# Routing of the first MoE: token numbers kept in SBUF and stored once, half-width one-hots, gathers issued ahead of weights

## The chip, the cores and the metric

The kernel runs on one core of a Trainium2 chip. The metric is the device time of one execution in microseconds (us), as the median of several runs.

## The reference

Three stages run one after the other on 2 x 768 tokens of width 512 in float32: attention with 4 sink positions and a window of 128, a greedy mixture of experts (MoE), and a second MoE that mixes all experts with Sinkhorn weights. The change is in the greedy routing of the first MoE:

```python
logits = x @ w_gate                       # 1536 tokens, 8 experts
order = np.argsort(-logits.flatten())
for idx in order:                         # best (token, expert) pair first
    tok, e = idx // E, idx % E
    if assigned[tok] >= 0 or counts[e] >= cap:   # cap = 1536 / 8 = 192
        continue
    assigned[tok] = e; counts[e] += 1
for e in range(E):
    mask = assigned == e
    out[mask] = np.maximum(x[mask] @ w1[e], 0) @ w2[e]   # w1 512x1024, w2 1024x512
```

The second MoE takes `out` for all 1536 tokens; the kernel computes it in slot order (expert by expert) and scatters the rows to their tokens at the very end.

## The kernel before

Attention writes its rows to a DRAM tile `X` in chunks of 128 tokens and counts the first routing round along the way (`cnt0`). Then `routing_and_moe1` runs eight rounds. A round finds which expert fills up next and fixes its 192 tokens:

- `count(n, m, prop, row)` (L550 to L572) counts, for each token, how many tokens that propose the same expert stand before it. VectorE builds comparison matrices `g` and `gt` (L559 to L562, four buffers each, `GB = 4`), TensorE multiplies them with the proposals (L568), in groups of two chunks (`GC = 2`). There are n = 12 chunks in rounds 0 to 3 and, after `compact`, n = 6 in rounds 4 to 7. Round 0 takes `cnt0` and needs no count.
- `route(r)` (L574 to L606) picks the expert: `sel`, `red`, two small matmuls into `sm` (L590, L591), then `t1`, `eh`, `fin`, `ft`. At its end it strikes the expert and the placed tokens from `val` (L604, L605).
- `place_tokens(r, ...)` (L608 to L633) writes the expert's number to `EIX`, starts the weight loads (`load_w`, L648, 1 MB each, four for an expert: two halves of w1, two of w2), works out each token's slot (L611 to L613), builds one-hot rows `oh` of 192 columns (L617), multiplies them with the tokens' two-part number `code` (L622, a 2 x 192 result), folds the two parts and turns them to 96 partitions with four small matmuls against `pw` (L626, L629), casts them to the index tile `ix` (L631), and calls `gather`.
- `gather(r)` (L651 to L660) fetches 2 x 96 rows of `X` on the POOL queue (L657) and stores the 192 indices to the DRAM tile `idxd` on the SP queue (L660). Each index is an element of its own in DRAM, 4 bytes long.
- `propose()` (L527 to L546) makes the next round's proposals and spreads the values `m` along rows with TensorE (`bc`, L544) and ScalarE (`row`, L545).

`turn_tokens(r)` (L684 to L696) transposes the gathered rows into `xe`. `moe1(r)` (L698 to L733) multiplies: 64 instructions of L708 for w1, 64 of L719 for w2; half way through its L719 part it turns the tokens of round r + 1. The weights lie in six buffers of 1 MB (`WB = 6`). For round 0 w1 is loaded on the SP queue, w2 on the ACT queue after the last `row` copy (`st["shown"]`), and `turn_tokens(0)` is held until the third group of round 1's count (`KC = 2`).

A planner orders each engine's instructions from the program's order and its own costs. The routing has high priority; `tc.issue_after(x)` holds an instruction behind `x`. So routing of round r + 1 runs on VectorE while TensorE works on `moe1(r)`, and TensorE's order is fixed when the kernel is built.

`moe2` starts with a load of all indices from `idxd` to `ixo` (L793), used only by the scatters at the end (L875). Its weights come in halves of 512 KB on the SP queue (L437, L461), into three buffers (`SB = 3`), well ahead of use.

Of the kernel before, what the change touches and what calls it, by code (L numbers as in the profile page):

```python
# [20 lines left out]
def kernel(  # L21
# [21 lines left out]
    P = 128  # L43
# [27 lines left out]
    EIX = consts.tile([P, E], I32, name="EIX")  # L71

# [9 lines left out]
    slots = rp.tile([P, CAP], BF, name="slots")  # L82
    nc.vector.tensor_scalar(slots, place[:, :CAP], 5001.0, None, op0=OP.add)
# [4 lines left out]
    nc.gpsimd.iota(tok[:, :, 0], pattern=[[1, NCH]], base=0, channel_multiplier=0)  # L88
# [13 lines left out]
    HC = CAP // 2  # L102
    jw = rp.tile([2, 1], I32, name="jw")
    nc.gpsimd.iota(jw, pattern=[[0, 1]], base=P, channel_multiplier=1 - P)
    pw = rp.tile([2, 1], F32, name="pw")
    nc.vector.tensor_copy(pw, jw)
# [364 lines left out]
    def routing_and_moe1():  # L471
# [16 lines left out]
        IDX = {}  # L488
# [39 lines left out]
        def propose():  # L528
            n, L, val = st["n"], st["L"], st["val"]
            mx = rp.tile([P, n], F32, name="mx", bufs=2)  # L530
            prop = rp.tile([P, n, E], BF, name="prop", bufs=2)
            pl = rp.tile([P, n, E], F32, name="pl", bufs=2)
            m = rp.tile([P, n], F32, name="m", bufs=2)
            bc = lambda a: a.unsqueeze(2).to_broadcast([P, n, E])
            nc.vector.tensor_reduce(mx, val, axis=AX.X, op=OP.max)
            nc.vector.scalar_tensor_tensor(prop, val, 0.0, bc(mx), op0=OP.max, op1=OP.is_equal)
            nc.vector.tensor_mul(pl, prop, L)
            nc.vector.tensor_reduce(m, pl, axis=AX.X, op=OP.add)
            row = rp.tile([P, n, P], F32, name="row", tag="row", bufs=1)
            for c0 in range(0, n, 4):  # L540
                pb = ps.tile([P, 4, P], F32, name="bc", bufs=2)
                c1 = min(n, c0 + 4)
                for c in range(c0, c1):
                    nc.tensor.transpose(pb[:, c - c0, :], m[:, c:c + 1].to_broadcast([P, P]), ident)  # L544
                shown = nc.scalar.activation(row[:, c0:c1, :], pb[:, :c1 - c0], AF.Copy)  # L545
            st.update(row=row, m=m, prop=prop, shown=shown.ins)  # L546

        def count(n, m, prop, row):

            cnt = ps.tile([P, n, E], F32, name="cnt", bufs=1)  # L550
            nc.tensor.matmul(cnt.rearrange("p c e -> p (c e)"), zb, zb[:, :n * E], start=True, stop=False,
                             skip_group_check=True)
            for c0 in range(0, n, GC):
                c1 = min(n, c0 + GC)
                blocks = []
                for c in range(c0, c1):
                    g = gp.tile([P, n, P], BF, name="g", bufs=GB)
                    gt = gp.tile([P, P], BF, name="gt", bufs=GB)
                    nc.vector.scalar_tensor_tensor(gt, row[:, c], m[:, c:c + 1], before, op0=OP.is_equal, op1=OP.mult)  # L559
                    nc.vector.tensor_scalar(g[:, :c + 1], row[:, :c + 1], m[:, c:c + 1], None, op0=OP.is_lt)  # L560
                    if c + 1 < n:
                        nc.vector.tensor_scalar(g[:, c + 1:], row[:, c + 1:], m[:, c:c + 1], None, op0=OP.is_le)  # L562
                    blocks += [(c, gt, prop[:, c, :])] + [(cc, g[:, cc, :], prop[:, c, :]) for cc in range(n)]

# [6 lines left out]
                st.setdefault("counted", []).append(mm.ins)  # L571
            return cnt  # L572

        def route(r):  # L574
            n, L, val, code, m, prop = (st[x] for x in ("n", "L", "val", "code", "m", "prop"))
            bc = lambda a: a.unsqueeze(2).to_broadcast([P, n, E])
# [25 lines left out]
            ft = rp.tile([P, 2, n], F32, name="ft", bufs=2)  # L602
# [3 lines left out]
            return cnt, fin, ft, t1, code, n  # L606

        def place_tokens(r, cnt, fin, ft, t1, code, n):  # L608
            nc.vector.tensor_scalar(EIX[:, r:r + 1], t1[:, 1:2], -1.0, float(E), op0=OP.mult, op1=OP.add)
            load_w(r, (0,) if r == 0 else (0, 1))  # L610
            nc.vector.tensor_mul(fin, fin, cnt)  # L611
            nc.vector.tensor_reduce(ft[:, 1], fin, axis=AX.X, op=OP.add)
            nc.vector.tensor_add(ft[:, 1], ft[:, 0], ft[:, 1])  # L613
            sm = ps.tile([P, 512], F32, name="sm", bufs=1)
            ohs = gp.tile([P, n, CAP], BF, name="oh", bufs=OB)
            for c in range(n):
                nc.vector.tensor_scalar(ohs[:, c], slots, ft[:, 1, c:c + 1], None, op0=OP.is_equal)  # L617

            first = None
            for c in reversed(range(n)):  # L620
                with nullcontext() if first is None else tc.issue_after(first.ins):
                    mm = nc.tensor.matmul(sm[:2, :CAP], code[:, c, :], ohs[:, c], start=(c == n - 1), stop=(c == 0),  # L622
                                          skip_group_check=True)
# [8 lines left out]
            IDX[r] = ix  # L632
            gather(r)  # L633

        W, XG, YT = {}, {}, {}
        JH = KF // 2
        KC = 2
# [3 lines left out]
        def load_w(r, mats=(0, 1), q=nc.sync):  # L641
            e = q.value_load(EIX[0:1, r:r + 1], min_val=0, max_val=E - 1)
            for a in mats:
                src = (moe_w1, moe_w2)[a][bass.ds(e, 1)].rearrange("o (k p) f -> p (o k) f", p=P)
                for h in range(2):
                    t = bp.tile([P, WT], F32, name="wf", tag="w", bufs=WB)
                    t = t.rearrange("p (k f) -> p k f", f=DM if a else F // 2)
                    q.dma_start(t, src[:, h * KF // 2:(h + 1) * KF // 2] if a  # L648
                                else src[:, :, h * F // 2:(h + 1) * F // 2])
                    W.setdefault(r, ([], []))[a].append(t)  # L650

        def gather(r):
            ix = IDX[r]
            XG[r] = []
            for a in range(2):
                t = mp.tile([P, DM], F32, name=f"xg{a}", bufs=1)
                nc.gpsimd.indirect_dma_start(out=t[:HC], out_offset=None, in_=X[:, :],  # L657
                                             in_offset=bass.IndirectOffsetOnAxis(ap=ix[:, a:a + 1], axis=0))
# [26 lines left out]
        def turn_tokens(r):  # L685
# [3 lines left out]
            with tc.issue_after(st["counted"][KC]) if r == 0 else nullcontext():  # L689
                for k0 in range(0, KD, 2):  # L690
                    pt = pm.tile([P, 2, CAP], F32, name="mm", tag="mm", bufs=3)
                    for k in (k0, k0 + 1):
                        for a in range(2):
                            nc.tensor.transpose(pt[:, k - k0, a * HC:(a + 1) * HC], xg[a][:HC, k * P:(k + 1) * P],
                                                ident[:HC, :HC])
                    nc.scalar.activation(xe[:, k0:k0 + 2, :], pt, AF.Copy)  # L696

# [37 lines left out]
        for r in range(E):  # L735
            with tc.high_priority(offset=HP):
                got = route(r)
                place_tokens(r, *got)
                if r + 1 == E // 2:
# [10 lines left out]
            if r == 1:  # L750
                turn_tokens(0)
# [8 lines left out]
    def moe2(cx):  # L760
# [30 lines left out]
        acc = cp.tile([P, NCH, DM], F32, name="accs")  # L791
        ixo = cp.tile([P, NCH], I32, name="ixo")
# [146 lines left out]
```

## Time and profile before

| | |
|---|---|
| median of 3 runs | 1435.92 us (1433.2 to 1439.34) |
| the profiled execution | 1440.94 us |
| its span in the trace | 1439.2 us |
| TensorE busy in the span | 1394.8 us, 97% |
| mean granted TensorE clock | 0.979 of full speed |

The span runs from the first to the last instruction of the program; the profiled execution's time is 1.74 us longer. Attention takes the first 157 us, routing and the first MoE lie from 157 to about 415, the second MoE from there to the end. A granted clock of 1.00 is 2.4 GHz, 0.50 is 1.2 GHz.

### The profile page before, as it was taken

The page shows a single profiled execution, that of the slowest core. Times are in us where ns is not written, and L with a number is a line of the kernel's source. Part 1 is how long each engine was busy: PE and PEld are TensorE (multiplying, and loading weights), DVE is VectorE, ACT ScalarE, POOL GpSimd, SP SyncE. Part 2 cuts the span into 40 slices and gives each one's busy share as a digit, 9 for nine tenths or more (in the row PEclk, how much of TensorE's full clock was granted, in tenths as well). Part 3 has the DMA queues.
Part 4 walks back from the last instruction along what each step waited for, and adds up shares of the span by engine and source line. Part 5 has one row for each costly group of instructions (what it writes and reads, how often), then busy time and mean ns, then how long its engine had stood idle before and what let it go on. Part 6 is the DMA issues. An engine that isn't in the chain of part 4 may idle for free.

```text
span 1439.2 us, 20856 instructions
## 1 busy us (share of the span) xinstructions
PE 1394.8 (97%) x8275; PEld 1233.9 (86%) x8275; DVE 839.0 (58%) x1875; ACT 460.9 (32%) x975; POOL 412.0 (29%) x389
## 2 busy tenths in 40 slices
PE   7999589999989999999999999999999999999998
PEld 4667489999987988888898888888889888889887
DVE  4766767673156755555555555555555555555554
ACT  4566111221233322332333333233233333323321
POOL 1136200010252332243232234323223423222403
PEclk9999689999999999999999999999999999999999
DMA  6331453387620010011001001001100100100002
GB/s 128 94 82 38 87 185 129 129 182 152 224 59 15 30 44 30 30 41 34 30 30 45 30 31 44 30 30 41 34 30 30 45 30 30 44 30 30 15 1 88
DMA packets 87338, 87.39 MB, mean 61 GB/s; under 512 B 43976, under 2 KB 60360, under 8 KB 87240
## 3 DMA queue, kind: packets, MB, share of 16 engines
q1 hardware_dynamic: 82696, 74.50, 17.7%
q0 software_dynamic: 2944, 9.44, 3.2%
q10 hardware_dynamic: 1600, 2.11, 0.4%
q8 instruction: 65, 1.06, 0.3%
q14 instruction: 33, 0.27, 0.1%
HBM read 79.75 MB, written 6.30 MB: 60 GB/s over the span
## 4 chain that ended last, share of the span: by engine, by line
PE 91%; DVE 3%; DMA 2%; issue 2%; ACT 1%; POOL 0%; SPq 0%; POOLq 0%; DVEq 0%; ACTq 0%
PE pa L862 37%; PE X L805 18%; PE Z L805 9%; PE mm L719 5%; PE mm L708 5%; PE Y L805 5%; PE S L241 2%; DMA xg<-X,ix 2%; PE o L296 2%; PE PT L283 1%; PE ms L308 1%; PE cnt L568 1%; PE tr L217 1%; ACT pb L254 1%; PE lg L730 1%
## 5 line engine op out<-in xcount | busy, mean ns | idle before, releaser
L862 PE MATMUL pa<-w,h 128*128 128x512 f32 x2304 | 597.1, 395 | 0.0
L862 PEld LDWEIGHTS pa<-w,h 128*128 128x128 f32 x2304 | 427.7, 188 | 67.7 <-ACT h L812 0.3
L873 DVE SCALAR_TENSOR_TENSOR accs<-pa,Pm,accs 128x512 f32<-128x512 f32 x360 | 269.1, 747 | 212.0 <-PE pa L862 211.4
L813 DVE SCALAR_TENSOR_TENSOR h<-sum,h 128x384 fp32r<-128x384 f32 x192 | 156.1, 813 | 99.2 <-ACT h L812 99.0
L447 POOL TENSOR_TENSOR w1l<-r,w1h 128x512 fp32r<-128x512 f32 x64 | 64.6, 1031 | 446.0 <-ACT w1h L446 416.1
L812 ACT ACTIVATE h<-sum 128x384 fp32r<-128x384 f32 x192 | 100.4, 523 | 208.0 <-DVE sum L822 207.9
L464 POOL TENSOR_TENSOR w<-r,w 128x1024 fp32r<-128x1024 f32 x32 | 77.3, 2417 | 232.8 <-ACT w L463 232.8
L817 ACT ACTIVATE u<-X 128x384 f32<-128x384 f32 x64 | 31.5, 492 | 268.6 <-PE X L805 268.6
L708 PE MATMUL mm<-xe,wf 128*128 128x192 f32 x512 | 96.6, 340 | 0.0
L719 PE MATMUL mm<-hT,wf 128*128 128x192 f32 x512 | 96.0, 337 | 0.0
L447 POOL TENSOR_TENSOR w1l<-S,w1h 128x1024 fp32r<-128x1024 f32 x32 | 86.9, 2714 | 0.0
L708 PEld LDWEIGHTS mm<-xe,wf 128*128 128x128 f32 x512 | 84.9, 195 | 0.9 <-issue 0.3
L719 PEld LDWEIGHTS mm<-hT,wf 128*128 128x128 f32 x512 | 84.5, 194 | 0.8 <-issue 0.2
L657 POOL DMA_INDIRECT xg<-X,ix x16 | 16.3, 1020 | 192.6 <-DVE ix L631 126.7
L822 DVE TENSOR_TENSOR sum<-Z,u 128x384 f32<-128x384 f32 x64 | 35.7, 557 | 58.8 <-ACT u L817 58.8
L817 ACT ACTIVATE v<-X 128x384 f32<-128x384 f32 x64 | 31.4, 491 | 78.0 <-PE X L805 78.0
L254 ACT ACTIVATE pb<-pb,nb 128x264 f32<-128x264 f32 (+1 forms) x96 | 46.4, 488 | 14.5 <-DVE nb L249 13.3
L813 DVE SCALAR_TENSOR_TENSOR h<-X,h 128x384 fp32r<-128x384 f32 x64 | 35.7, 558 | 21.8 <-ACT h L812 21.8
L822 DVE TENSOR_TENSOR sum<-Z,v 128x384 f32<-128x384 f32 x64 | 35.7, 557 | 18.6 <-PE Z L805 18.5
L812 ACT ACTIVATE h<-X 128x384 fp32r<-128x384 f32 x64 | 31.5, 492 | 46.0 <-PE X L805 45.9
L446 ACT ACTIVATE w1h<-r 128x512 fp32r<-128x512 f32 x64 | 30.0, 516 | 49.3 <-PE Z L805 46.2
L244 DVE CUSTOM_DVE_ANT_0 pb<-S,M 128x264 f32<-128x264 f32 (+1 forms) x96 | 36.5, 403 | 14.4 <-PE S L241 13.7
(284 smaller groups left out, 2362.0 us busy)
## 6 DMA issues: line engine op xcount, KB each, us to landing
r<-in_moe_w_dram SPq DMA_DIRECT2D x64, 512.0 KB, 3.5
wf<-in_moe_w_dram SPq DMA_DIRECT2D x30, 1024.0 KB, 5.4
kn<-in_k_dram SPq DMA_DIRECT2D x12, 256.0 KB
qn<-in_q_dram SPq DMA_DIRECT2D x12, 256.0 KB, 4.4
vn<-in_v_dram SPq DMA_DIRECT2D x12, 256.0 KB, 3.1
X<-xs POOLq DMA_DIRECT2D x12, 256.0 KB, 2.6
wf<-in_moe_w_dram ACTq DMA_DIRECT2D x2, 1024.0 KB
xg<-X,ix POOLq DMA_INDIRECT x16, 8.2
```

Of the source, the lines that this page charges most:

```text
L254: nc.scalar.activation(PB[c][:, h, :w], PB[c][:, h, :w], AF.Exp, bias=NB[c][:, 0, h:h + 1], scale=scale, accum_out=NB[c][:, 2, h:h + 1])
L447: nc.gpsimd.tensor_sub(w1[1][:, o:o + n], x, w1[0][:, o:o + n].bitcast(F32))
L464: nc.gpsimd.tensor_sub(w2[:, 1], r2, w2[:, 0].bitcast(F32))
L708: nc.tensor.matmul(ph[:, j - j0, :], w1[j // JH][:, k, j % JH * P:(j % JH + 1) * P], xe[:, k, :], start=(k == 0), stop=(k == KD - 1))
L719: nc.tensor.matmul(py[:, k - k0, :], w2[j // JH][:, j % JH, k * P:(k + 1) * P], hT[:, j, :], start=(j == 0), stop=(j == KF - 1))
L805: nc.tensor.matmul(acc_, w1[a][:, o, k, :], XO[x][t][b][:, k, :], start=(start and n == 0), stop=(stop and n == 3 * KH - 1), skip_group_ch ...
L812: nc.scalar.activation(t[:, 0], x, AF.Relu)
L813: nc.vector.scalar_tensor_tensor(t[:, 1], x, 0.0, t[:, 0].bitcast(F32), op0=OP.max, op1=OP.subtract)
L817: nc.scalar.activation(t, x, AF.Copy)
L822: nc.vector.tensor_add(t, a, b)
L862: nc.tensor.matmul(pa, HT[u, f, h][:, a, j * P:(j + 1) * P], w2[:, b, f, :], start=(n == 0), stop=(n == 3 * FP - 1))
L873: nc.vector.scalar_tensor_tensor(acc[:, c], pa, pe, acc[:, c], op0=OP.mult, op1=OP.add)
```

## The change

Six edits, all around the routing:

1. The one-hots have 96 columns. A token's slot is split into its half (`ft[:, 1]`, 0 or 1) and its place in the half (`ft[:, 2]`). The one-hots stand as weights on TensorE and the token numbers move past them, four columns for each chunk (`ch`: two parts of the number, for each half). The result lies on 96 partitions at once: a reduction adds the two parts and a cast writes `ixs[:, r, :]`. The copy `fi`, the four matmuls against `pw` and the tile `pw` are gone. `code` holds 128 x chunk in its first part, so no factor is needed.
2. The slot number comes from `fin = (cnt + 1) * fin`, built in `route`; two operations and an addition in `place_tokens` are gone.
3. The eight stores to `idxd` are gone. `moe2` stores all 1536 indices once, ahead of the load to `ixo`.
4. In rounds 1 to 7 the gathers stand ahead of the weight loads, which are held until the indices are known. In round 0 the first half of w1 is loaded ahead; the other three halves are on the ACT queue after the last `row` copy.
5. The striking of expert and tokens from `val` is a function of its own (`leave`), after the placing.
6. On TensorE the `bc` transposes are held behind the placing matmuls; `turn_tokens(0)` is called in round 0 and held behind the last `bc` transpose, and round 1's count is held behind it.

```diff
         nc.vector.scalar_tensor_tensor(fin, cnt, float(CAP) - 0.5, prop, op0=OP.is_lt, op1=OP.mult)
+        nc.vector.scalar_tensor_tensor(fin, cnt, 1.0, fin, op0=OP.add, op1=OP.mult)
...
-        nc.vector.scalar_tensor_tensor(val, be(eh), -100.0, val, op0=OP.mult, op1=OP.add)
-        nc.vector.scalar_tensor_tensor(val, bc(ft[:, 0]), -1000.0, val, op0=OP.mult, op1=OP.add)
...
-        nc.vector.tensor_scalar(EIX[:, r:r + 1], t1[:, 1:2], -1.0, float(E), op0=OP.mult, op1=OP.add)
-        load_w(r, (0,) if r == 0 else (0, 1))
-        nc.vector.tensor_mul(fin, fin, cnt)
-        nc.vector.tensor_reduce(ft[:, 1], fin, axis=AX.X, op=OP.add)
-        nc.vector.tensor_add(ft[:, 1], ft[:, 0], ft[:, 1])
+        if r == 0:
+            expert()
+            load_w(0, ((0, 0),))
+        nc.vector.tensor_scalar(ft[:, 1], ft[:, 0], HC + 0.5, None, op0=OP.is_gt)
+        nc.vector.scalar_tensor_tensor(ft[:, 2], ft[:, 1], -float(HC), ft[:, 0], op0=OP.mult, op1=OP.add)
         sm = ps.tile([P, 512], F32, name="sm", bufs=1)
-        ohs = gp.tile([P, n, CAP], BF, name="oh", bufs=OB)
+        ohs = gp.tile([P, n, HC], BF, name="oh", bufs=OB)
         for c in range(n):
-            nc.vector.tensor_scalar(ohs[:, c], slots, ft[:, 1, c:c + 1], None, op0=OP.is_equal)
+            nc.vector.tensor_scalar(ohs[:, c], slots, ft[:, 2, c:c + 1], None, op0=OP.is_equal)
+        ch = gp.tile([P, n, 2, 2], BF, name="ch", bufs=OB)
+        nc.vector.tensor_mul(ch[:, :, 1], code, ft[:, 1].unsqueeze(2).to_broadcast([P, n, 2]))
+        nc.vector.tensor_sub(ch[:, :, 0], code, ch[:, :, 1])
...
-                mm = nc.tensor.matmul(sm[:2, :CAP], code[:, c, :], ohs[:, c], start=(c == n - 1), stop=(c == 0),
-                                      skip_group_check=True)
+                mm = nc.tensor.matmul(sm[:HC, 0:4], ohs[:, c], ch[:, c].rearrange("p h a -> p (h a)"),
+                                      start=(c == n - 1), stop=(c == 0), skip_group_check=True)
...
-        fi = rp.tile([2, CAP], F32, name="fi", bufs=2)
-        nc.vector.tensor_copy(fi, sm[:2, :CAP])
-        sm = ps.tile([P, 512], F32, name="sm", bufs=1)
-        for a in range(2):
-            nc.tensor.matmul(sm[:HC, a:a + 1], fi[:, a * HC:(a + 1) * HC], pw, start=True, stop=True)
-        ix = rp.tile([HC, 2], I32, name="ix", bufs=3)
-        nc.vector.tensor_copy(ix, sm[:HC, 0:2])
+        st["placed"] = mm.ins
+        at = rp.tile([HC, 2], F32, name="at", bufs=2)
+        nc.vector.tensor_reduce(at, sm[:HC, 0:4].rearrange("p (h a) -> p h a", h=2), axis=AX.X, op=OP.add)
+        known = nc.vector.tensor_copy(ixs[:, r, :], at)
         gather(r)
+        if r:
+            with tc.issue_after(known.ins):
+                expert()
+            load_w(r, PARTS)
...
+    def leave(ft, eh, n):
+        val = st["val"]
+        nc.vector.tensor_scalar(ft[:, 3], ft[:, 0], 0.5, None, op0=OP.is_gt)
+        nc.vector.scalar_tensor_tensor(val, eh.unsqueeze(1).to_broadcast([P, n, E]), -100.0, val, op0=OP.mult,
+                                       op1=OP.add)
+        nc.vector.scalar_tensor_tensor(val, ft[:, 3].unsqueeze(2).to_broadcast([P, n, E]), -1000.0, val,
+                                       op0=OP.mult, op1=OP.add)
...
-        nc.sync.dma_start(idxd[r * CAP:(r + 1) * CAP, :].rearrange("(a p) o -> p (a o)", p=HC), ix)
...
             place_tokens(r, *got)
+            leave(got[0], got[2], got[4])
...
                 with tc.issue_after(st["shown"]):
-                    load_w(0, (1,), nc.scalar)
+                    load_w(0, PARTS[1:], nc.scalar)
+                turn_tokens(0)
...
-        if r == 1:
-            turn_tokens(0)
...
     acc = cp.tile([P, NCH, DM], F32, name="accs")
+    nc.sync.dma_start(idxd.rearrange("(r a p) o -> p (r a o)", a=2, p=CAP // 2), ixs.rearrange("p r a -> p (r a)"))
     ixo = cp.tile([P, NCH], I32, name="ixo")
     nc.sync.dma_start(ixo, idxd.rearrange("(c p) o -> p (c o)", p=P))
```

## Rows read from the trace of the kernel before

**Rows 1.** The page: busy time, share of the span, instructions.

```profile
PE 1394.8 (97%) x8275; PEld 1233.9 (86%) x8275; DVE 839.0 (58%) x1875; ACT 460.9 (32%) x975; POOL 412.0 (29%) x389
```

**Rows 2.** Windows: one expert's stretch; length, busy by engine, granted clock, DMA share, GB/s.

```profile
347.10:369.65 22.55, 22.55 (x146) 22.43 (x146) 1.19 (x3) 4.65 (x11) 2.57 (x3) 1.00 0.82 238
```

**Rows 3.** Chain that ended last, 130 to 460 us: start, length, what.

```profile
162.77 2.25 DVE oh L617 x12
165.06 2.08 PE sm L622 x12
...
169.11 10.02 DMA xg<-X,ix
...
202.44 7.66 DMA xg<-X,ix
...
211.36 0.67 PE cnt L568 x26
212.29 4.30 PE mm L719 x14
...
217.22 2.06 PE mm L719 x12
...
233.67 1.08 PE sm L622 x12
...
235.44 0.42 PE sm L629 x4
...
291.33 0.59 PE sm L622 x6
```

**Rows 4.** Timeline of round 0, 150 to 232 us: start, length, instruction.

```profile
160.97 0.24 DVE L603 TENSOR_REDUCE ft<-fin 128x12 f32<-128x96 f32 x1
...
162.78 1.08 SPq L648 DMA_DIRECT2D wf<-in_moe_w_dram  x2
...
168.67 0.15 DVE L631 CAST ix<-sm 96x2 int32<-96x2 f32 x1 [1.15 <-PE sm L629]
...
169.69 0.35 DVE L559 SCALAR_TENSOR_TENSOR gt<-row,m,before 128x128 bf16<-128x128 f32 x1 [0.87 <-ACT row L545]
...
170.40 0.60 ACT L545 ACTIVATE row<-bc 128x512 f32<-128x512 f32 x1 [0.25 <-PE bc L544]
...
170.45 0.93 POOL L657 DMA_INDIRECT xg<-X,ix  x1 [0.30 <-issue]
...
171.96 0.98 ACTq L648 DMA_DIRECT2D wf<-in_moe_w_dram  x2
...
182.33 2.93 PE L708 MATMUL mm<-xe,wf 128*128 128x192 f32 x8
```

**Rows 5.** DMA queues, 171 to 180 us: packets, MB, share of 16 engines.

```profile
q0 software_dynamic: 101, 0.33, 74.6%
q10 hardware_dynamic: 57, 0.12, 8.4%
```

**Rows 6.** DMA queues, 365 to 369 us.

```profile
q0 software_dynamic: 128, 0.39, 33.2%
```

**Rows 7.** Line L660, the eight stores to idxd: issue to landing.

```profile
DMA to landing us min/median/max: 11.0/11.9/12.7
```

**Rows 8.** Timeline of TensorE: its waits for gathered rows in moe1(0) and moe1(1).

```profile
208.00 0.30 PE L694 MATMUL mm<-ident,xg 96*128 96x96 f32 x1 [1.65 <-DMA xg<-X,ix]
210.14 1.22 PE L694 MATMUL mm<-ident,xg 96*128 96x96 f32 x6 [1.84 <-DMA xg<-X,ix]
...
245.09 0.80 PE L694 MATMUL mm<-ident,xg 96*128 96x96 f32 x7 [0.86 <-DMA xg<-X,ix]
```

**Rows 9.** Timelines of SP and ACT in the second MoE.

```profile
424.99 0.50 SPq L793 DMA_DIRECT2D ixo<-idxd  x1
...
451.33 0.37 SPq L461 DMA_DIRECT2D r<-in_moe_w_dram  x1
...
500.99 1.06 ACT L463 ACTIVATE w<-r 128x1024 fp32r<-128x1024 f32 x1 [0.89 <-PE pa L862]
```

More of the change, by code (lines that the diff above doesn't have):

```diff
@@ L81 @@
     nc.vector.tensor_copy(place, ji)
-    slots = rp.tile([P, CAP], BF, name="slots")
-    nc.vector.tensor_scalar(slots, place[:, :CAP], 5001.0, None, op0=OP.add)
+    HC = CAP // 2
+    slots = rp.tile([P, HC], BF, name="slots")
+    nc.vector.tensor_scalar(slots, place[:, :HC], 5001.0, None, op0=OP.add)
     je = rp.tile([P, E], I32, name="je")
@@ L543, in propose @@
                 for c in range(c0, c1):
-                    nc.tensor.transpose(pb[:, c - c0, :], m[:, c:c + 1].to_broadcast([P, P]), ident)
+                    with tc.issue_after(st["placed"]):
+                        spread = nc.tensor.transpose(pb[:, c - c0, :], m[:, c:c + 1].to_broadcast([P, P]), ident)
                 shown = nc.scalar.activation(row[:, c0:c1, :], pb[:, :c1 - c0], AF.Copy)
-            st.update(row=row, m=m, prop=prop, shown=shown.ins)
+            st.update(row=row, m=m, prop=prop, shown=shown.ins, spread=spread.ins)
         def count(n, m, prop, row):
             cnt = ps.tile([P, n, E], F32, name="cnt", bufs=1)
-            nc.tensor.matmul(cnt.rearrange("p c e -> p (c e)"), zb, zb[:, :n * E], start=True, stop=False,
-                             skip_group_check=True)
+            turned = st.pop("turned", None)
+            with nullcontext() if turned is None else tc.issue_after(turned):
+                nc.tensor.matmul(cnt.rearrange("p c e -> p (c e)"), zb, zb[:, :n * E], start=True, stop=False,
+                                 skip_group_check=True)
             for c0 in range(0, n, GC):
@@ L601, in route, with place_tokens, expert @@
             nc.vector.tensor_mul(fin, fin, be(eh))
[L602 removed]
+            ft = rp.tile([P, 4, n], F32, name="ft", bufs=2)
             nc.vector.tensor_reduce(ft[:, 0], fin, axis=AX.X, op=OP.add)
[L604 to L613 removed]
+            return ft, t1, eh, code, n
+        def place_tokens(r, ft, t1, eh, code, n):
+            def expert():
+                return nc.vector.tensor_scalar(EIX[:, r:r + 1], t1[:, 1:2], -1.0, float(E), op0=OP.mult, op1=OP.add)
+            if r == 0:
[3 more added lines that the diff above has]
+            nc.vector.scalar_tensor_tensor(ft[:, 2], ft[:, 1], -float(HC), ft[:, 0], op0=OP.mult, op1=OP.add)
             sm = ps.tile([P, 512], F32, name="sm", bufs=1)
[L615 removed]
+            ohs = gp.tile([P, n, HC], BF, name="oh", bufs=OB)
             for c in range(n):
[L617 removed]
+                nc.vector.tensor_scalar(ohs[:, c], slots, ft[:, 2, c:c + 1], None, op0=OP.is_equal)
+            ch = gp.tile([P, n, 2, 2], BF, name="ch", bufs=OB)
+            nc.vector.tensor_mul(ch[:, :, 1], code, ft[:, 1].unsqueeze(2).to_broadcast([P, n, 2]))
+            nc.vector.tensor_sub(ch[:, :, 0], code, ch[:, :, 1])
             first = None
@@ L635, in routing_and_moe1, with load_w @@
         W, XG, YT = {}, {}, {}
         JH = KF // 2
-        KC = 2
+        PARTS = ((0, 0), (0, 1), (1, 0), (1, 1))
         GC, GB = 2, 4
         OB = 1
-        def load_w(r, mats=(0, 1), q=nc.sync):
+        def load_w(r, parts, q=nc.sync):
             e = q.value_load(EIX[0:1, r:r + 1], min_val=0, max_val=E - 1)
-            for a in mats:
+            for a, h in parts:
                 src = (moe_w1, moe_w2)[a][bass.ds(e, 1)].rearrange("o (k p) f -> p (o k) f", p=P)
[L645 to L650, printed above, removed]
+                t = bp.tile([P, WT], F32, name="wf", tag="w", bufs=WB)
+                t = t.rearrange("p (k f) -> p k f", f=DM if a else F // 2)
+                q.dma_start(t, src[:, h * KF // 2:(h + 1) * KF // 2] if a else src[:, :, h * F // 2:(h + 1) * F // 2])
+                W.setdefault(r, ([], []))[a].append(t)
@@ L688, in turn_tokens @@
             xe = XE[r] = mp.tile([P, KD, CAP], F32, name="xe", bufs=1)
-            with tc.issue_after(st["counted"][KC]) if r == 0 else nullcontext():
+            with tc.issue_after(st["spread"]) if r == 0 else nullcontext():
                 for k0 in range(0, KD, 2):
```

22 lines of the change are left out of this document (7 added, 15 removed).

## The prediction

> **What bounds the kernel now.** I read the page first: TensorE is busy for 97% of the span [rows 1]. That is an average, so I went to the windows of one expert at a time: from 347 to 370 us, where no routing is left, TensorE is busy for all of its 22.55 us at the full clock [rows 2]. There only less work on TensorE helps. Then I read the chain that ended last over the routing stage. Round 0 is different: the chain runs through VectorE's one-hots, the placing matmuls and then 10.02 us of one gather [rows 3]. The timeline shows the first matmul of the first MoE only at 182.33 us, 8 of them taking 2.93 us, the half clock [rows 4]. TensorE's own timeline names its last waits: 1.65 and 1.84 us for round 1's rows, 0.86 us for round 2's [rows 8]. Behind the first two, 14 matmuls take 4.30 us, where 12 take 2.06 a little later [rows 3]: the clock fell to its lower level after the wait. So a gain can come from three places: the start at 182.33 us, these waits, and TensorE's routing work.
>
> **Why the gather of round 0 takes 10 us.** The queues from 171 to 180 us tell it. The gather's queue moves 0.33 MB and keeps the engines for 74.6% of 9 us; the weights that ACT issued at 171.96 us move 0.12 MB [rows 4, 5]. In round 7 a whole gather of 0.39 MB takes 33.2% of 4 us [rows 6]: for each MB 3.4 us of all engines instead of 20. What differs: in round 0 the 192 single-index stores went out just ahead of the gather, and such a store takes 11.0 to 12.7 us to land [rows 7], so until about 180 us. Round 7's gather has no store ahead of it. My reading is that the stores in flight slow all that comes behind, the gather and w2 alike.
>
> **Round 0, step by step.** The count's `ft` is reached at 160.97 + 0.24 = 161.2 us as before; the added (cnt + 1) * fin falls into VectorE's wait for the `sm` matmuls. Now the one-hots begin at 162.77 [rows 3, 4]. After the change two short dependent operations stand between, about 0.2 us each like `ft`: one-hots from 161.65. Twelve take 2.25 us [rows 3], 0.19 each; at half the width each lies between half of that and the same, I take 0.15: 1.8 us, to 163.45. The two operations on `ch`: 0.35, to 163.8. The placing matmuls become 12 short ones with 4 columns. Nearest are the count's 26 in 0.67 us at full clock [rows 3], so 0.3 us, double at the lower clock; the old 2.08 us is the upper bound. I take 0.6: 164.4. Reduction and cast take the place of copy, fold and cast, two VectorE operations, 0.4 us: 164.8. Before, the cast ended at 168.67 + 0.15 = 168.8. So indices come **4.0 us earlier**.
>
> The gathers start at 165.1 and, 1.3 us apart as before (169.11 and 170.45) [rows 3, 4], 166.4. With no store in flight I price a gather by round 7, within 4 us [rows 6], and take 3: rows at 169.4 us. The other bound is the old price, 170.45 to about 181, which is a rival below. ACT comes next: the last `row` copy ended at 171.0 [rows 4]. The proposals start after the placing as before, the first `g` on VectorE moves from 169.69 [rows 4] to about 167.1, so the last copy ends at 168.4. ACT needed 1.0 us to issue the first load and 0.98 for two, so three are out at 170.9, and only then does it copy `xe`. The first matmul of moe1(0) starts at 172.0 instead of 182.33: **-10.3 us**. Between -8 (ACT or the gather a little late) and -12 (the copies planned ahead of the loads). The second half of w1 is now behind the gather: issued at 169.4, it needs to be there after 32 matmuls at 0.17 to 0.37 us [rows 3, 4], after 177 us at the earliest, so it is hidden if the ACT queue flows at once.
>
> **Rounds 1 and later.**
> Gather waits of round 1: the count starts 2.6 us earlier, isn't held up by much else, and the same savings between `sel` and the indices are about 2.4 us. By this the rows of round 1 come about 12 us earlier than at 210.1, and TensorE, which is 10.3 us ahead, needs them about when they come. Of 1.65 + 1.84 us I leave 0.5: **-3.0**. With the wait gone the half clock behind it goes too, 14 matmuls at 2.06/12 are 2.4 instead of 4.30: **-1.9**. Round 2's 0.86 us: **-0.9** [rows 3, 8].
> TensorE's work: L622 takes 1.08 us in rounds 1 to 3 and 0.59 in rounds 4 to 7 [rows 3]; new 0.31 and 0.15 by the count's price. 3 x 0.77 + 4 x 0.44 = 4.1. The four fold matmuls go, 0.42 in each of 7 rounds [rows 3]: 2.9. Together **-7.0**, all on the path, since TensorE is the bound there.
> Against it: three of round 1's six count groups ran while TensorE waited for round 0's rows. Now all stand behind `turn_tokens(0)`, 3 x 0.67: **+2.0**. VectorE holds four `g` buffers, so it works on for some 5 us past 167.1 and isn't stopped before the count begins at about 170.6.
> Costed at nothing: `leave` and the extra VectorE operations (as many go as come, and VectorE idles while TensorE multiplies); weights later by some 6 us in rounds 1 to 7, since 1 MB halves already wait for a free buffer in most rounds, and round 1's are needed only at about 207 us; without these covers each late half would stop TensorE for as long as it is late.
>
> **The store at the second MoE.** It is 1536 single elements, issued at about 404 us (424.99 less 21), and the load to `ixo` waits for it on SP. Behind it in SP's queue stands the w2 half of 451.33, which ACT first uses at 500.99 [rows 9]. So SP can be held for some 70 us at no cost. Nothing in the trace has so many stores in one; lower bound, one old store's 11 to 13 us (hidden), upper bound eight of them, 88 to 102 us [rows 7]. The old stores went to one 768-byte piece each, these go to all pieces at once, so I take the low end.
>
> **Sum.** -10.3 - 3.0 - 1.9 - 0.9 - 7.0 + 2.0 = -21.1 us. From the profiled execution's 1440.94 that is 1419.8. It lies 5.0 us above the median 1435.92; the median after comes to **1415 us**, 1.5% faster.
>
> **Rivals.**
> *Gather stays slow.* The 10 us belong to the first gather and not to the stores. Then the rows come at 177 us, the start moves by 4 us only: 1421 us. For it: in round 1 a gather takes 7.66 us too [rows 3]. Against: that one had 4 MB of weights ahead, and round 7. Chance 0.14.
> *Order is worth nothing.* In round 1 the gather's packets still share the engines with weights that are issued 1 us later; wait and lower clock stay: 3.0 + 1.9 back, 1420 us. The Trainium skill, DMA: Bandwidth & Descriptors, section "Issuing engines are not separate DMA queues", says that DMAs of all issuing engines run on the same 16 and interleave. By that rule the order of issue buys little here; the 7.66 us agree with it. Chance 0.15.
> *The one store is slow.* It costs by the element: 88 to 102 us hold SP from 404 to 492 or 506. The w2 half then comes 16 to 30 us after ACT wants it, and ACT, in order, stops the products: 1431 to 1445 us. From 93 us on it takes more than the 21 that were won, and the kernel is slower; at 102 by 0.6%. It would be worse if the planner issued it early among the last weights. The Trainium skill, same page, "Specifications", speaks for it: below 512 B a write is a read-modify-write. By that each of the 1536 pays, and the estimate is the upper end. Rows 7 agree that single elements are dear, and can't say whether the price adds up. Chance 0.11.
> *The planner's order.* Tokens of round 0 ahead of the count hold TensorE and the count longer than thought, or the lower clock comes back elsewhere at 2 us a time: 1423 to 1434 us. Chance 0.08.
>
> **From cases to numbers.** The forecast has 0.52 (own range 1408 to 1421; the low side is a start 12 us earlier and no wait at all). A measurement here can tell about 0.5%, 7 us, from no change. Faster by more (under 1428.7): 0.52 + 0.14 + 0.15 and half of the last case, 0.85. Within it: half of the store's case and the rest of the last, 0.09. Slower: 0.06, the store's upper end. For 8 in 10 the range takes in the two near rivals and the last one's lower part, 1404 to 1430.
>
> **What would show it.** Right: gathers of round 0 landing within 4 us, the first L708 near 172 us, no wait for `xg` over 0.5 us in moe1(0), no 14-matmul stretch of 4.3 us behind it, the placing groups at 0.3 and 0.15 us, no gap on SP that reaches ACT's L463. Wrong: a gather that still takes 10 us, ACT's loads that sit 8 us in their queue, or SP standing at `ixo` while weights are due.

## Result, and the profile after

After the change the kernel takes **1415.21 us** (median of 4 runs, 1413.82 to 1420.05) against 1435.48 us for the kernel before on the same chip: ratio 0.9862, interval 0.9843 to 0.988. The profiled execution has a span of 1413.8 us where that of before has 1439.2. The 25.4 us between these two spans are looked for below; the medians differ by 20.3, so some 5 us of what the two traces differ by belongs to the two executions.

The busy line of the page of the changed kernel:

```profile
PE 1375.5 (97%) x8243; PEld 1221.7 (86%) x8243; DVE 835.5 (59%) x1898; ACT 459.8 (33%) x975; POOL 411.8 (29%) x388
```

TensorE has lost 19.3 us of work against [rows 1], so most of the gain is work or lower clock that is gone and not idle time. Where it went is read from the windows of one expert at a time. First before, moe1(0), moe1(1) and moe1(4), and the first 45 us of the second MoE (columns: window, its length, busy time of TensorE, its weight loads, VectorE, ScalarE, GpSimd with counts, granted clock, DMA share, GB/s):

```profile
182.33:221.03 38.70, 35.21 (x355) 33.35 (x354) 24.91 (x75) 6.13 (x13) 2.20 (x2) 0.87 0.43 151
221.03:253.70 32.67, 31.81 (x363) 30.32 (x363) 25.05 (x76) 6.76 (x14) 2.20 (x2) 1.00 0.42 142
...
316.60:347.10 30.50, 30.50 (x226) 28.70 (x227) 16.86 (x71) 7.07 (x16) 1.93 (x2) 0.94 0.79 150
414.48:460.00 45.52, 39.01 (x184) 34.12 (x184) 35.59 (x88) 17.34 (x34) 17.73 (x15) 0.87 0.13 35
```

And the same stretches of the changed kernel, with the one ahead of its first matmul of moe1(0):

```profile
157.00:177.00 20.00, 9.36 (x136) 7.93 (x137) 16.45 (x58) 2.66 (x5) 1.96 (x2) 0.50 0.59 207
177.09:208.41 31.32, 31.32 (x358) 30.25 (x355) 26.93 (x83) 5.73 (x12) 1.83 (x2) 0.95 0.44 162
208.41:239.46 31.05, 31.05 (x364) 30.05 (x364) 24.46 (x80) 6.82 (x15) 1.98 (x2) 1.00 0.44 150
...
297.46:323.65 26.19, 26.19 (x212) 25.80 (x212) 13.26 (x53) 6.74 (x16) 4.75 (x6) 1.00 0.67 203
...
391.01:436.00 44.99, 38.39 (x188) 33.31 (x188) 35.75 (x89) 17.34 (x34) 17.70 (x15) 0.93 0.13 36
```

moe1(0) starts 5.2 us earlier (177.09 for 182.33), is 7.4 us shorter and without a gap on TensorE (31.32 busy in 31.32; 35.21 in 38.70 before). These windows end up to 0.9 us off an expert's first w1 matmul; counted from first w1 matmul to first w1 matmul, moe1(0) is 7.7 us shorter, moe1(1) to moe1(4) are 2.0, 2.1, 2.1 and 4.3 us shorter, and the last three experts the same. In moe1(4) the clock was 0.94 and is 1.00. The rest of the span is some 2 us shorter, its first 45 us at clock 0.93 instead of 0.87.

Of the 5.2 us, 2.3 are none of the change's: the routing's first reduction on TensorE (`sm<-red`) begins at 156.36 instead of 158.64, and that moment lies between 154.8 and 159.0 in the profiles of all the kernels here, with edits that don't touch what stands ahead of it. So the start is worth 3.0 us (23.7 us behind the routing's start before, 20.7 now), not 10.3. The timeline of that stretch shows why:

```profile
163.31 0.16 DVE L632 CAST ixs<-at 96x2 int32<-96x2 f32 x1
164.32 1.03 POOL L668 DMA_INDIRECT xg<-X,ixs  x1 [9.33 <-DVE m L534]
165.66 0.93 POOL L668 DMA_INDIRECT xg<-X,ixs  x1 [0.30 <-issue]
168.39 1.52 ACTq L661 DMA_DIRECT2D wf<-in_moe_w_dram  x3
168.83 1.22 PE L704 MATMUL mm<-ident,xg 96*128 96x96 f32 x6 [0.75 <-DMA xg<-X,ixs]
169.96 0.87 ACT L706 ACTIVATE xe<-mm 128x384 f32<-128x384 f32 x2 [2.54 <-PE mm L704]
...
173.73 0.48 PE L568 MATMUL cnt<-prop,g 128*128 128x8 bf16 x12 [1.78 <-DVE g L562]
176.37 0.48 PE L568 MATMUL cnt<-prop,g 128*128 128x8 bf16 x12 [1.78 <-DVE g L562]
...
177.09 2.91 PE L720 MATMUL mm<-xe,wf 128*128 128x192 f32 x8
```

The second gather goes out at 165.66 and TensorE turns its rows at 168.83: the 10.02 us of [rows 3] became 3. `xe` is ready at 170.8. But TensorE doesn't begin moe1(0) then: between the turned rows and the first L720 stand 104 count matmuls, four of round 1's six groups, and they wait for VectorE's `g`. Its own list of waits from 140 to 440 us:

```profile
PE cnt L568 <- DVE g L562: 3.9, 3, 1.8
...
PE mm L704 <- DMA xg<-X,ixs: 1.5, 2, 0.8
```

Both waits for rows are round 0's; those of [rows 8] are gone. VectorE's timeline shows what the count ahead of moe1(0) does for it. In the kernel before it waited twice for TensorE's count, 5.9 us in all; in the changed kernel it waits once, 1.90 us:

```profile
185.62 0.35 DVE L559 SCALAR_TENSOR_TENSOR gt<-row,m,before 128x128 bf16<-128x128 f32 x1 [2.45 <-PE cnt L568]
...
191.65 0.26 DVE L585 SCALAR_TENSOR_TENSOR sel<-cnt,prop 128x96 f32<-128x96 f32 x1 [3.43 <-PE cnt L568]
```

From the routing's start to round 1's indices it took 42.3 us before (200.94 less 158.64) and takes 34.2 now (190.53 less 156.36). Not all of these 8.1 us are the count's: with the old placing put back (old_placing below) it takes 38.3.

The placing itself, from TensorE's groups by line: first before, 182 to 400 us (busy us, mean ns), then after, 177 to 400 us, the same 60 matmuls.

```profile
L629 PE MATMUL sm<-pw,fi 2*96 2x1 f32 x28 | 3.5, 223 | 0.0
L622 PE MATMUL sm<-oh,code 128*2 128x192 bf16 x36 | 3.5, 246 | 0.0
L622 PE MATMUL sm<-oh,codec 128*2 128x192 bf16 x24 | 2.6, 245 | 0.0
```

```profile
L626 PE MATMUL sm<-ch,oh 128*96 128x4 bf16 x60 | 3.5, 182 | 0.1
```

9.6 us became 3.5: 6.1 us less on TensorE.

### The profile page after: what moved, and what is told of

The parts are those of the page before. It is cut to its first block, busy times and chain, and to the rows that moved or that the text cites. A ratio compares the mean times of both kernels' runs of the same rounds, so it can differ in the third digit from the quotient of the medians.

```text
span 1413.8 us, 20799 instructions
## 1 busy us (share of the span) xinstructions
PE 1375.5 (97%) x8243; PEld 1221.7 (86%) x8243; DVE 835.5 (59%) x1898; ACT 459.8 (33%) x975; POOL 411.8 (29%) x388
## 4 chain that ended last, share of the span: by engine, by line
PE 93%; DVE 4%; ACT 1%; issue 1%; POOL 0%; DMA 0%; SPq 0%; POOLq 0%; DVEq 0%; ACTq 0%
PE pa L875 37%; PE X L818 19%; PE Z L818 9%; PE mm L720 6%; PE mm L731 6%; PE Y L818 5%; PE S L238 2%; PE o L293 2%; PE PT L280 1%; PE cnt L568 1%; PE ms L305 1%; PE tr L214 1%; PE lg L742 1%; POOL out_dram L888 0%; ACT pb L251 0%
## 5 line engine op out<-in xcount | busy, mean ns | idle before, releaser
L720 PE MATMUL mm<-xe,wf 128*128 128x192 f32 x512 | 95.9, 337 | 0.0
L731 PE MATMUL mm<-hT,wf 128*128 128x192 f32 x512 | 91.5, 331 | 0.0
L720 PEld LDWEIGHTS mm<-xe,wf 128*128 128x128 f32 x512 | 83.1, 192 | 0.1
L668 POOL DMA_INDIRECT xg<-X,ixs x16 | 16.7, 1041 | 168.3 <-PE mm L704 60.6
L826 DVE SCALAR_TENSOR_TENSOR h<-X,h 128x384 fp32r<-128x384 f32 x64 | 35.7, 558 | 21.1 <-ACT h L825 21.1
## 6 DMA issues: line engine op xcount, KB each, us to landing
wf<-in_moe_w_dram ACTq DMA_DIRECT2D x3, 1024.0 KB, 10.3
```

The source lines that it names most:

```text
L720: nc.tensor.matmul(ph[:, j - j0, :], w1[j // JH][:, k, j % JH * P:(j % JH + 1) * P], xe[:, k, :], start=(k == 0), stop=(k == KD - 1))
L731: nc.tensor.matmul(py[:, k - k0, :], w2[j // JH][:, j % JH, k * P:(k + 1) * P], hT[:, j, :], start=(j == 0), stop=(j == KF - 1))
L826: nc.vector.scalar_tensor_tensor(t[:, 1], x, 0.0, t[:, 0].bitcast(F32), op0=OP.max, op1=OP.subtract)
```

## Experiments

The ratios are against the kernel before on the same chip; the changed kernel stands at 0.9862, and run again beside two of the others at 0.9856 (0.9831 to 0.9881).

### Do single-index stores slow the gather?

**stores_adjacent**: the changed kernel, with the per-round stores back, into a DRAM tile that nothing reads.

```
+    side = dram.tile([N, 1], I32, name="side")
...
+            nc.sync.dma_start(side[r * CAP:(r + 1) * CAP, 0:1].rearrange("(a p) o -> p (a o)", p=HC), ixs[:, r, :])
```

> The changed kernel, plus in every round the old store of the 192 indices, 4 bytes each, side by side in DRAM, issued on SP behind the gathers, to a tile that nobody reads. If stores in flight are what slowed the gather of round 0: its rows land 10 to 12 us after issue instead of 3.1, the first matmul of the first MoE comes 5 to 8 us later, and the kernel is 4 to 8 us slower than the changed one (about 1420 to 1423 us). If the gather is quick now only because fewer weights stand ahead of it: rows still within 4 us, and within 2 us of the changed kernel.

**stores_spread**: the same stores, each index 512 bytes from the next.

```
-    side = dram.tile([N, 1], I32, name="side")
+    side = dram.tile([N, 128], I32, name="side")
```

> The same added stores, but each of the 192 indices 512 bytes from the next in DRAM. If the price of a store lies in 4-byte writes that share a stretch of DRAM: the gather of round 0 lands within 4 to 5 us and the kernel is within 2 us of the changed one. If it lies in the number of small writes: as with the stores side by side, 10 us or more for the gather and 4 to 8 us slower.

Measured: 1442.51 us (ratio 1.0024, 1.0008 to 1.004) with the adjacent ones, 1417.62 (0.9852, 0.983 to 0.9875) with the spread ones. In rounds 0 to 3 the store is issued on SP 0.7 to 0.8 us ahead of the first gather. The chain that ended last, with the adjacent stores, shows one gather of each of the rounds 0 to 3:

```profile
165.73 10.48 DMA xg<-X,ixs
...
200.27 14.46 DMA xg<-X,ixs
...
237.06 14.72 DMA xg<-X,ixs
...
272.10 14.43 DMA xg<-X,ixs
```

Landing times of the gathers from 155 to 262 us, as far as this view has them (rounds 1 and 2), adjacent and then spread:

```profile
DMA to landing us min/median/max: 12.4/13.4/14.7
```

```profile
DMA to landing us min/median/max: 4.9/6.2/7.5
```

192 words side by side make it two to three and a half times as long (13.4 for 6.2 at the median, 10.48 for 3.1 in round 0); the same 192 words 512 bytes apart do nothing. So it is neither the count of the elements nor their size: it is single words written into one stretch of DRAM. The DMA views of round 1 say where the time goes. First the microsecond in which the adjacent words are written (packets under 512 bytes), then 7 us that begin 3 us later, adjacent and spread:

```profile
DMA packets 208, 0.00 MB, mean 1 GB/s; under 512 B 208, under 2 KB 208, under 8 KB 208
```

```profile
DMA packets 112, 0.24 MB, mean 34 GB/s; under 512 B 0, under 2 KB 0, under 8 KB 112
```

```profile
DMA packets 1159, 2.46 MB, mean 351 GB/s; under 512 B 63, under 2 KB 63, under 8 KB 1158
```

The words themselves are out within 1 us. What comes behind them, gather and weights alike, then moves at 34 GB/s instead of 351. The prediction's reading of round 0 is shown. The size in later rounds was not foreseen: TensorE waits 20.7 us for rows, and all of the gain and more is lost.

### Do gathers ahead of weights matter?

**weights_first**: edit 4 undone for rounds 1 to 7.

```
-            if r == 0:
-                expert()
-                load_w(0, ((0, 0),))
+            expert()
+            load_w(r, PARTS if r else ((0, 0),))
```

> The changed kernel with the weight loads of rounds 1 to 7 ahead of the gathers again, as soon as the expert is known. If the order matters: round 1's rows land about 7.5 us after issue instead of 6.3, TensorE waits 1 to 3 us for them in moe1(0), the lower clock may follow (2 us): 1 to 4 us slower. If the gathers share the engines with the weights anyway: within 1 us of the changed kernel.

Measured: 1416.47 us (0.9845, 0.9825 to 0.9864), the same as the changed kernel, no wait for rows after round 0, gathers of rounds 1 and 2 at 6.0 to 7.1 us. By itself the order is worth nothing: over rounds 1 and 2 a gather takes 6.5 us at the median with gathers ahead (the changed kernel run again) and 6.5 with weights ahead. The Trainium skill, DMA: Bandwidth & Descriptors, section "Issuing engines are not separate DMA queues", says that DMAs of all issuing engines run on the same 16 engines and interleave; these traces agree.

**adjacent_weights_first**: both of these edits in one kernel.

> The changed kernel with the added stores of indices side by side in every round (which made it 25 us slower) and with the weights of rounds 1 to 7 ahead again (which alone changed nothing). If the old order shielded the gathers, since a store behind 4 MB of weights in SP's queue reaches DRAM after the gather: in rounds 1 to 3 the rows land 7 to 8 us after issue instead of 14.5, only round 0 keeps its 10 us, and the kernel is at 1421 to 1428 us, 15 to 20 us faster than with the stores alone. If the stores do their harm whatever stands ahead: 1438 us or more.

Measured: 1423.61 us (0.9915, 0.989 to 0.994). Round 0's gather takes 8.38 us, round 2's 7.0 and 7.3. With weights ahead in SP's queue the adjacent stores cost 7 us by the medians and 10 by the ratios, with gathers ahead some 24. In the old order each store stands behind 4 MB of weights in that queue, and its words are written only when the rows have been moved: here the gather's 0.39 MB of round 1 (`q0`) go from 200 to 205 us and the words from 205 to 206.

```profile
q0 software_dynamic: 128, 0.39, 21.2%
```

```profile
DMA packets 320, 0.23 MB, mean 226 GB/s; under 512 B 210, under 2 KB 210, under 8 KB 320
```

So edits 3 and 4 hang together. Edit 4 alone, on the kernel before, would by this cost time; that kernel was not run.

### What is each part worth?

**before_one_store**: the kernel before with edit 3 alone.

```
-            ix = rp.tile([HC, 2], I32, name="ix", bufs=3)
-            nc.vector.tensor_copy(ix, sm[:HC, 0:2])
-            IDX[r] = ix
+            nc.vector.tensor_copy(ixs[:, r, :], sm[:HC, 0:2])
+            IDX[r] = ixs[:, r, :]
...
-            nc.sync.dma_start(idxd[r * CAP:(r + 1) * CAP, :].rearrange("(a p) o -> p (a o)", p=HC), ix)
```

> The kernel before with one edit alone: no store of the indices in the rounds, one store at the second MoE. In the kernel before, the stores of rounds 1 to 3 stand behind 4 MB of weights in SP's queue, so they reach DRAM after the gathers, and only round 0's harms. If that is so: round 0's rows land within 4 us of issue, but TensorE still runs three count groups first (to 178.8 us), so the first matmul comes about 2 us earlier and the kernel gains 2 to 4 us only. Rival, that the stores are worth in the kernel before what they cost in the changed one: 20 us or more.

Measured: 1432.41 us (0.9959, 0.9942 to 0.9976), 5.9 us faster, more than the 2 to 4 expected. Round 0's gather falls to 3.13 us here too, with the weights ordered as before, yet the first matmul of moe1(0) stands 22.1 us behind the routing's start, where it stood 23.7 behind: 7 us of gather give 1.6 us of start. TensorE's waits for rows are 3.7 us here and 6.1 before; what else makes up the 5.9 is open.

**old_placing**: the changed kernel with one-hots of 192 columns, the copy and the fold.

```
-                    mm = nc.tensor.matmul(sm[:HC, 0:4], ohs[:, c], ch[:, c].rearrange("p h a -> p (h a)"),
-                                          start=(c == n - 1), stop=(c == 0), skip_group_check=True)
+                    mm = nc.tensor.matmul(sm[:2, :CAP], code[:, c, :], ohs[:, c], start=(c == n - 1), stop=(c == 0),
+                                          skip_group_check=True)
```

> The changed kernel with the old placing alone put back: one-hots of 192 columns, the fold by four small matmuls, its copy and cast. The working of the prediction: 7.0 us of TensorE's work come back in rounds 1 to 7, and the indices of round 0 come 2 to 3 us later, so 8 to 10 us slower than the changed kernel. Rival, that TensorE's small matmuls hide behind its waits for VectorE: 2 to 3 us slower.

Measured: 1428.58 us (0.9922, 0.9898 to 0.9946). The difference of the ratios, 0.006, makes the placing worth about 9 us, as expected. 6.1 us of it are TensorE's work. The indices come later too, round 1's 38.3 us behind the routing's start instead of 34.2; that the rest of the 9 lies there is likely and not shown.

**order_undone**: edit 6 undone.

```
-                    with tc.issue_after(st["placed"]):
+                    if True:
...
-            with tc.issue_after(st["spread"]) if r == 0 else nullcontext():
+            with tc.issue_after(st["counted"][2]) if r == 0 else nullcontext():
...
+            if r == 1:
+                turn_tokens(0)
```

> The changed kernel with its order of TensorE's work undone (the tokens of round 0 turned behind round 1's third count group, the bc transposes held behind nothing, round 1's count held behind nothing). If moe1(0) is bound by VectorE's comparisons, which come in the same rhythm either way: within 2 us of the changed kernel. If the order won the start, as the prediction's step has it: the first matmul of moe1(0) 2 us or more later and the kernel slower by as much.

Measured: 1415.57 us (0.9854, 0.9833 to 0.9875). Nothing. Three groups of the count are ahead of the tokens again, waits for `g` are 5.6 us in place of 3.9, and in the trace the experts from moe1(1) on start 0.9 us later behind the routing's start, which the time doesn't show. The first matmul of moe1(0) stands 20.8 us behind it, as in the changed kernel (20.7): the count waits for VectorE's `g` in either order.

### Would an earlier start of moe1(0) pay?

**fill**: moe1(0)'s w1 matmuls go between round 1's count groups, 32 in all, so that they fill the waits for `g`.

```
+                for _ in range(FILL.pop(0) if "fill" in st and FILL else 0):
+                    with tc.issue_after(mm.ins):
+                        last = next(st["fill"])
...
+        FILL = [1, 1, 2, 2, 2]
```

> The changed kernel with 32 of the 64 w1 instructions of moe1(0) put between round 1's count groups by hand (4, 4, 8, 8, 8), where TensorE waits 3.9 us for VectorE and where the planner put four count groups ahead of the first of them. If the planner's order is what held the start: the first such matmul at about 171 us after a routing that starts at 156.4, 3 to 4 us won over the changed kernel, less what TensorE then waits for round 1's rows, whose gather was only 1 us ahead of it: 1 to 4 us faster. If VectorE's comparisons bound moe1(0) anyway: within 1 us.

Measured: 1423.54 us (0.9892, 0.9875 to 0.9909), some 4 us slower than the changed kernel. The first matmul is 14.3 us behind the routing's start in place of 20.7, as meant. Then TensorE stands in front of round 1's rows. Its timeline, and the window behind it:

```profile
198.04 0.42 PE L711 MATMUL mm<-ident,xg 96*128 96x96 f32 x1 [3.45 <-DMA xg<-X,ixs]
```

```profile
198.00:204.00 6.00, 5.80 (x69) 5.54 (x70) 3.72 (x9) 0.98 (x2) 0.00 (x0) 0.50 1.05 397
```

3.45 us of wait and then 6 us at half clock, with round 2's count behind the rows in TensorE's order: round 2's indices come 69.0 us behind the routing's start, 61.7 in the changed kernel. Round 1's come 35.0 us behind it, 34.2 in the changed kernel: the start doesn't move them.

**fill_late**: fill, with round 1's rows turned at the end of moe1(0)'s w2 part.

```
-                if k0 == 0 and r + 1 < E:
+                if k0 == (0 if r else KD - 2) and r + 1 < E:
```

> The kernel with the w1 instructions put between the count groups, where TensorE waited 3.45 us for round 1's rows with the lower clock behind it, and now the turning of round 1's rows stands a quarter of moe1(0) later, behind all of its w2 part. If that wait is what ate the earlier start: no wait for rows in moe1(0), 3 to 5 us faster than the changed kernel (1410 to 1412 us). If the turned rows then come too late for moe1(1): a wait of TensorE for ACT's copy of 1 to 2 us, and 1 to 3 us won.

Measured: 1416.18 us (0.9854, 0.9832 to 0.9875): the same as the changed kernel, where 3 to 5 us were expected. The start is 6.5 us earlier, but part of that is only an exchange of places with the count. What is won are the 3.7 us of waits for `g` that are gone; moe1(1) begins 3.0 us earlier, and the lead is 1.5 at moe1(3) and 0.5 at moe1(5). Two things eat it. One is a new wait of 1.1 us for round 2's rows, whose indices come at the same time as ever (62.2 us behind the routing's start, 61.7 in the changed kernel). The other is the clock: in both kernels it is granted at 0.50 up to 180 us, and with the earlier start more of moe1(0)'s w1 matmuls fall into that stretch. Their 64, changed kernel and then fill_late (window, its length, busy time of these alone, clock, DMA share, GB/s):

```profile
177.09:208.27 31.18, 13.32 (x64) 11.38 (x65) 0.95 0.44 163
173.20:207.90 34.70, 14.95 (x64) 12.41 (x64) 0.89 0.59 221
```

That is 1.6 us more. Of the 1.0 us that remains of the 3.7, half is still there at moe1(5).

**vector_more**: four more VectorE operations, 1 us each, in round 1's count; nothing reads them.

```
+                    if "turned" not in st and "extra" not in st and c in (3, 5, 7, 9):
+                        idle = gp.tile([P, NCH * P], BF, name="idle", bufs=1)
+                        nc.vector.tensor_scalar(idle, row.rearrange("p c q -> p (c q)"), m[:, c:c + 1], None,
+                                                op0=OP.is_lt)
```

> The changed kernel with four more VectorE operations of 1.0 us each in round 1's count alone (comparisons into a tile that nobody reads). If VectorE's chain to round 1's indices is what TensorE meets in moe1(0) (the rows were there only 1 us before they were needed): round 1's indices 4 us later, TensorE waits 3 us for rows, and the kernel is 3 to 6 us slower than the changed one. If TensorE's own work is the only bound there: within 1 us.

Measured: 1427.36 us (0.9953, 0.9935 to 0.997), about 13 us slower by the ratios where 3 to 6 were expected. Round 1's indices come 39.6 us behind the routing's start, 5.4 late, and TensorE's timeline has the wait:

```profile
205.51 0.41 PE L709 MATMUL mm<-ident,xg 96*128 96x96 f32 x1 [3.39 <-DMA xg<-X,ixs]
```

The direction agrees with VectorE's chain as a limit close at hand in the first rounds. The size does not settle it: in this kernel the planner also put round 2's count behind the turned rows, as in fill, so that delay is in the 13 us (round 2's indices come 11.8 us late).

### Weights held back until the rows are there

**fill_gate**: fill, with the weights of rounds 1 to 3 waiting for the gathered rows by way of GpSimd.

```
+                    nc.gpsimd.tensor_scalar(ef[:, 1:2], XG[r][1][0:1, 0:1], 0.0, None, op0=OP.mult)
+                    nc.gpsimd.tensor_add(ef[:, 2:3], ef[:, 0:1], ef[:, 1:2])
+                    nc.gpsimd.tensor_copy(EIX[0:1, r:r + 1], ef[:, 2:3])
```

> As with the matmuls put between the count groups, and in rounds 1 to 3 the weights are also held until the gathered rows have landed (the expert's number goes through GpSimd, which reads a gathered row). If the weights issued 1 us behind the gather are what makes it 6 us long instead of 3: rows of round 1 within 3.5 us of issue, and 1 to 3 us faster than with the first edit alone. If not, the same within 1 us, or slower where weights come late.

Measured: 1428.31 us (0.9917, 0.99 to 0.9933). The gathers of rounds 1 and 2 land in 3.1 to 3.7 us, where they took 6.5 to 7.5 in fill, so the weights issued right behind them are what doubles their time otherwise. But the weights came late, TensorE waited 10.3 us for them, and the kernel is slower than fill, where 1 to 3 us were to be won. GpSimd's timeline:

```profile
197.49 10.35 POOL L646 TENSOR_SCALAR ef<-xg 1x1 f32<-1x1 f32 x1 [2.90 <-DMA xg<-X,ixs]
207.93 2.06 POOL L647 TENSOR_TENSOR ef<-ef 1x1 f32<-1x1 f32 x1
...
237.17 0.41 POOL L646 TENSOR_SCALAR ef<-xg 1x1 f32<-1x1 f32 x1 [2.22 <-DMA xg<-X,ixs]
```

An operation on one element took 10.35 us in round 1 and 0.41 in round 2. VectorE was counting at the first time; the cause was not tried. The run shows the share of the weights in the gather's time, and no gain.

No kernel of these beats the changed one; stores_spread, weights_first, order_undone and fill_late equal it.

## Why the prediction was right, point by point

The time was met (1415 forecast), and so were the likeliest case and the mechanism of the stores. One term of the sum failed and others made up for it: that the sum came out is partly luck. In the profiled pair, from the routing's start to the first w1 matmul of the last expert, 21.2 us went where the sum has 21.1. But the start gave 7.3 us less than its term; moe1(0) gave 3.6 more than its terms, and moe1(1) to moe1(4) 10.5 where 6.7 were forecast (5.8 of placing and 0.9 of wait).

**Gather of round 0 and the stores: right.** Predicted 3 us, measured 3.1. The indices come at 163.5 instead of 168.8; without the attention's 2.3 us that is 3.1 us earlier, where 4.0 were forecast. Counted from the routing's start the rows are turned after 12.5 us, where 169.4 made it 10.8.

**The start, -10.3 us: the step that failed.** `xe` was ready at 170.8, 14.5 us behind the routing's start, where the forecast had the first matmul at 13.4 (172.0 less 158.64): rows and copy a little later than worked out. The larger error is another. The step "The first matmul of moe1(0) starts at 172.0 instead of 182.33" held the rows for the last thing that the first matmul waits for. In TensorE's order it was not: four count groups stood there, held up by VectorE, and the first matmul came 6.3 us after `xe`. The start moved by 3.0 us (5.2 with the attention). The term also counts a microsecond of start as one of time. In fill_late it was worth less, since the matmuls that came earlier fell into the stretch at clock 0.50.

**The count groups, +2.0, and the waits of round 1, -3.0 and -1.9.** The count groups were set behind the tokens, inside moe1(0), and made it longer; four in fact ran ahead of it, where three had. In exchange round 1's count held VectorE up less, its indices came 8.1 us earlier behind the routing's start (4.1 of that by the placing), and the waits of [rows 8] and the low clock behind them went whole. For moe1(0) the terms make -4.1 (-3.0 - 1.9 + 2.0 and 1.2 of placing); it was -7.7. Start and moe1(0) together: -14.4 forecast, -10.6 measured behind the routing's start.

Why a still earlier start pays so little: in the changed kernel TensorE itself ends last from 177 to 345 us, with less than 0.1 us of gaps, but VectorE's chain to the next indices is close behind. It takes some 27.5 us a round (indices at 163.3, 190.4, 217.9 and 245.9), TensorE 28 to 31 an expert. The second gathers of rounds 1 and 2 land at 199.1 and 227.0, and TensorE turns their rows here:

```profile
199.85 0.66 PE L704 MATMUL mm<-ident,xg 96*128 96x96 f32 x6
...
230.08 0.83 PE L704 MATMUL mm<-ident,xg 96*128 96x96 f32 x8
```

That leaves 0.7 and 3.1 us. A larger lead meets the rows: 3.45 us of wait in fill, 1.1 in fill_late.

**TensorE's work, -7.0: right in kind, a little large.** 6.1 us measured. The price taken from the count (0.31 for twelve) was too low: twelve take 0.50 to 0.55 us, six 0.23 to 0.39. Old_placing puts the whole of edit 1 at 9 us.

**Round 2's wait, -0.9: right.**

**The one store: hidden, as taken, but at another place.** The planner issued it at 314.75, among the last loads, and not at 404. The timeline of SP's and GpSimd's queue there:

```profile
314.75 0.42 SPq L804 DMA_DIRECT2D idxd<-ixs  x1
...
318.11 0.92 POOL L668 DMA_INDIRECT xg<-X,ixs  x1 [24.61 <-PE mm L704]
```

The DMA issues from 314 to 319 us, and from 319.3 to 320:

```profile
xg<-X,ixs POOLq DMA_INDIRECT x1, 10.2
...
xg<-X,ixs POOLq DMA_INDIRECT x1, 11.7
```

The two gathers of round 6, behind 1536 words, took 10.2 and 11.7 us, about the 10.02 of [rows 3] behind 192. They landed by 331.0, and their rows were needed only at 339.6: the prediction held an early place among the weights for the worse one, and here it was hidden. The load to `ixo` went out at 401.51, and no engine waited for a load in the second MoE. The slow store's rival took a row of the Trainium skill, DMA: Bandwidth & Descriptors, section "Specifications", on writes below 512 bytes for a price on each element. Stores_spread shows 192 such writes at no measurable cost, so here the size alone is not the price.

**Rivals.** The gather did not stay slow. "Order is worth nothing" was right for edits 4 and 6 taken by themselves (weights_first, order_undone) but not in its result: the waits went, since the indices came earlier, and the order did not matter. The planner's order did change the start, the failing step; fill_late, which takes most of the count out of the start's way, gains nothing.

**Not foreseen.** The stretch at half clock in moe1(4) is gone, and with it about 2 us; the first 45 us of the second MoE run at clock 0.93 for 0.87. No experiment aimed at either; in before_one_store moe1(4) runs at clock 1.00 too. The profiled execution of the kernel before lies 5 us above its median, and its other executions left no trace, so it isn't shown that these gains are the change's. With the attention's 2.3 us they are of the size of the 5 us by which the profiled span fell more than the median; that too is only a match of sizes.

## What to carry to other kernels

Ask of each engine what it still has to do in its own order between the event that comes earlier and the work that you hope to start; a faster transfer is worth only the time to the next thing in that order (here 3.0 of 10 us). Index lists that are written to DRAM word by word and side by side belong at a moment when no short transfer is under way, in one store, or spread. An edit that moves transfers can be harmful or free depending on what stood behind them in a queue: test such edits together and singly.

## What the hardware showed

- 192 adjacent 4-byte writes just ahead of a gather made it take 10.5 to 14.7 us in rounds 0 to 3, where it takes 3.1 to 8.4 in the changed kernel; 512 bytes apart they cost nothing. The words are out within 1 us; then all queues together moved 34 GB/s for 7 us instead of 351 (stores_adjacent, stores_spread, round 1).
- Behind 1536 adjacent ones in one store two gathers took 10.2 and 11.7 us, no multiple of what 192 do.
- Weights issued right behind a gather double its time: 3.1 to 3.7 us alone, 6.5 to 7.5 with them (fill_gate and fill, rounds 1 and 2).
- A one-element GpSimd operation took 10.35 us once and 0.41 a round later (fill_gate); why is open.
